# Second convolution of a spectral kernel: VectorE's chains on PSUM operands, SBUF sums on GpSimd, filters spread by DMA

## The chip, the core and the metric

The kernel runs on one core of one Trainium2 chip. The metric is the device time of one execution in microseconds (us); less is better.

## What is computed

The input x has 2 sequences of 3008 rows and 256 channels, in fp32. Three layers follow each other, and only the last one's result is handed out:

```python
X = np.fft.rfft(x, axis=1)
F = (filt_r + 1j * filt_i)[None, :, :]
y = np.fft.irfft(X * F, n=x.shape[1], axis=1).astype(np.float32)

x = y.reshape(6016, 256)
gate = 1.0 / (1.0 + np.exp(-(x @ w_gate)))        # 256 -> 1536
x = (gate * (x @ w_val) @ w_out).astype(np.float32)

h = x @ w_in                                      # 256 -> 2048
out = (h * (1.0 / (1.0 + np.exp(-1.702 * h))) @ w_out2).astype(np.float32)
```

## The kernel before

The Fourier transform of length 3008 = 47 x 64 is done as products with small tables. A convolution (class `Conv`) handles one sequence in 8 groups `g` of 32 channels, each group in two halves; a half is a chunk `j` = 2g + u with 16 channels, 16 chunks in all. For the second sequence (`b` = 1) its steps are:

- `a1(g)` (line 519): TensorE multiplies x with the table of length 47, in eight small matmuls of `four` (line 324), into PSUM banks 3 and 6. VectorE transposes both banks (line 526) into `a`. `highs` (ScalarE, 528) and `lows` (VectorE, 530) split `a` into a high and a low part `ap`, because a product in full precision is made of three matmuls (`mm3`, lines 124 to 126: high by high, high by low, low by high).
- `c1(j)` (532): the table of length 64, into bank 7. ScalarE copies the bank into `v` with real and imaginary halves exchanged (539, 540), VectorE multiplies the bank by the real filter into `y` (542), GpSimd multiplies `v` by the signed imaginary filter (543).
- `c1_sum(j)` (546): `y + v` on VectorE (548), high part `yp` on ScalarE (550), low part on VectorE (554).
- `d1(j)` (566): the inverse table of length 64, from `yp` into bank 7 again, and a transpose on VectorE into `z` (572).
- `e1(g)` (574): the inverse table of length 47, into banks 3 and 6, two transposes on VectorE into `tt` (408) and stores to memory.

`load_f(g)` (346) loads a group's two filters into partitions 0 to 63. `spread_f(j)` (394) copies each chunk's filters to partitions 64 to 127 on ScalarE (398), and `sign_f(j)` (400) multiplies the imaginary one by a table of signs on GpSimd (403).

This convolution is done inside 20 units of the second layer. A unit (loop at line 1194, `t` = 2, 3 and `f` = 2 to 11) takes one tile of 512 tokens and 128 columns of the hidden layer: six matmuls of the gate into one of PSUM banks 0 to 2, a sigmoid on ScalarE (1214), six of the value into another, their product on VectorE into `sg` (1247), a split into high part `g` (ScalarE, 120) and low part (GpSimd, 121), and six matmuls of `s12_back` (691) into banks 4 and 5, pushed back by two units (`depth`). Unit u carries `c1(u-1)`, `d1(u-2)`, and in alternation `a1` (even units) or `e1` (odd units).

Beside it the same units prepare what the third and later stages need: sums of the gate's weights (`combine_w1`, 1050, by `sum_ahead`), the split of tile 3 (657, 663), and the seven sums and differences of two later tiles ("forms", class `Forms`, 1083), each with a high part on ScalarE and a low part.

Each engine takes its instructions in the order in which this code lists them (`manual_schedule`, line 1181), and SyncE (SP) issues nearly all transfers from one queue, in that order as well.

Of the kernel before, what the change touches and what calls it, by code (L numbers as in the profile page):

```python
# [89 lines left out]
def kernel(  # L90
# [241 lines left out]
    class Conv:  # L332
        def __init__(self, b, fx, ff, fw):
            self.b, self.fx, self.ff, self.fw = b, fx, ff, fw
            self.x, self.f, self.st, self.z = {}, {}, {}, {}
            self.pa, self.pz, self.py = {}, {}, {}
            self.two = set()
            self.highs, self.lows = [], []
# [7 lines left out]
        def load_f(self, g):  # L346
            t = [self.ff.tile([P, 32, K1], F32, tag=f"f{i}", name=f"f{i}") for i in range(2)]
            gs = slice(g * 32, (g + 1) * 32)
            if self.b:
                for i in range(2):  # L350
                    nc.sync.dma_start(out=t[i][:64], in_=fd[i, :, gs])
            else:
                nc.sync.dma_start(out=t[0][:64], in_=fd[0, :, gs])
                for h in range(2):
                    hs = slice(g * 32 + h * 16, g * 32 + h * 16 + 16)
                    nc.sync.dma_start(out=t[1][h * 64:(h + 1) * 64, :16], in_=fd[1, :, hs])
# [163 lines left out]
        def a1(self, g):  # L520
            banks = ps[3], ps[6]
            x = self.x[g]
            four(enumerate(banks), tbl("t1"), lambda r, k: x[64 * r:64 * r + N1P, k], N1P)
            for u in range(2):
                a = self.fw.tile([P, 16, 32], F32, tag="a", name="a", bufs=2)
                nc.vector.transpose(a.rearrange("p c k -> p (c k)"), banks[u])
                ap = self.pair([P, 16, K1], "ap", 4)
                self.highs.append(lambda ap=ap, a=a: nc.scalar.activation(out=ap[0], in_=a[:, :, :K1], func=AF.Copy))
                self.st[2 * g + u] = ap
                self.lows.append(lambda ap=ap, a=a: nc.vector.tensor_sub(ap[1], a[:, :, :K1], ap[0].bitcast(F32)))  # L530

        def c1(self, j):
            g, u = divmod(j, 2)
            px = ps[7][:, :384]
            mm3(px, tbl3("t2"), self.st[j], True, True)
            pxv = px.rearrange("p (c k) -> p c k", k=K1)
            fr, fi = (t[:, u * 16:u * 16 + 16] for t in self.f[g])
# [3 lines left out]
            y = self.fw.tile([P, 16, K1], F32, tag="y", name="y", bufs=2)  # L541
            nc.vector.tensor_mul(y, pxv, fr)  # L542
            nc.gpsimd.tensor_mul(v, v, fi)
            self.st[j] = y, v

        def c1_sum(self, j):
# [3 lines left out]
            nc.scalar.activation(out=yp[0], in_=y, func=AF.Copy)  # L550
            self.st[j] = yp

            def low():
                nc.vector.tensor_sub(yp[1], y, yp[0].bitcast(F32))  # L554

            self.lows.append(low)

        def low(self):
            if self.lows:
                self.lows.pop(0)()  # L560
# [5 lines left out]
        def d1(self, j, bank=7):  # L566
# [7 lines left out]
        def e1(self, g):  # L574
# [475 lines left out]
    def combine_w1(f, n, v, r, eng=nc.vector):  # L1050
# [22 lines left out]
        def lo(k):  # L1073
            nc.vector.tensor_sub(dst[k][1], r[:, k], dst[k][0].bitcast(F32))  # L1074
# [8 lines left out]
    class Forms:  # L1083
# [41 lines left out]
        def inplace(self):  # L1125
            sub = nc.vector.tensor_sub
# [39 lines left out]

    cur = np_
# [4 lines left out]
    def sum_ahead(f, u):  # L1172
        if not ahead:
            ws = new_parts()[0].bitcast(F32).rearrange("p a (b m) -> p a b m", m=P)
            ahead.update({k: combine_w1(k, 1, ws[:, 0:1], ws[:, 1:2]) for k in range(PRE)})
        ahead[f][u]()

    for f in range(PRE):
        for u in range(5):
            at_unit(4 + (5 * f + u) * 4 // 5, lambda f=f, u=u: sum_ahead(f, u))  # L1180
# [12 lines left out]
    pre = []  # L1193
    for t in range(2, 4):
        for f in range(FK, FC1):
            pg, pv = front_bank(), front_bank()
            m = tiles[t][3]
            c = unit - 1 if 0 <= unit - 1 < NCH else None
            a = 0 if unit == 1 else unit // 2 if unit and unit % 2 == 0 and unit // 2 < 8 else None
            if c is not None and unit > 2:  # L1200
                conv.c1(c)
            if unit == 3:
                conv.c1_sum(1)
                conv.low()
# [6 lines left out]
            if unit != 2:  # L1211
                conv.high()
            sg = work.tile([P, 512], F32, tag="sg", name="sg")[:, :m]
            nc.scalar.activation(out=sg, in_=pg[:, :m], func=AF.Sigmoid)
            if unit != 2:
                conv.high()
            if unit == 2:
                conv.c1(0)
                conv.high()
                conv.high()  # L1220
                ended[0](0)
                conv.low()
                ended[0](1)
            elif unit == 3:
                conv.d1(0, 3)
                conv.c1_sum(2)
                conv.low()
            elif unit > 3:
                if c is not None:
                    conv.c1_sum(c)  # L1230
                    if a is not None:
                        conv.low()
                if 0 <= unit - 2 < NCH:
# [549 lines left out]
```

## Time and profile before

| | |
|---|---|
| runs | 1160.48 us median of 3 (1160.44 to 1161.47) |
| profiled execution | 1162.36 us, of which the span is 1160.5 us |
| TensorE (PE) busy | 1135.2 us, 98% of the span |
| VectorE (DVE) busy | 724.0 us, 62% |
| ScalarE (ACT) busy | 657.7 us, 57% |
| GpSimd (POOL) busy | 415.6 us, 36% |

The span is the time from the first to the last instruction of the profiled execution. The 20 units lie between about 172 and 313 us; the first convolution lies before 60 us, and the rest is matmul stages. "L542" is line 542 of the kernel. An engine's idle time is put down to whatever it waited for last.

### The profile page before, as it was taken

The page shows a single profiled execution, that of the slowest core. Times are in us where ns is not written, and L with a number is a line of the kernel's source. Part 1 is how long each engine was busy: PE and PEld are TensorE (multiplying, and loading weights), DVE is VectorE, ACT ScalarE, POOL GpSimd, SP SyncE. Part 2 cuts the span into 40 slices and gives each one's busy share as a digit, 9 for nine tenths or more (in the row PEclk, how much of TensorE's full clock was granted, in tenths as well). Part 3 has the DMA queues.
Part 4 walks back from the last instruction along what each step waited for, and adds up shares of the span by engine and source line. Part 5 has one row for each costly group of instructions (what it writes and reads, how often), then busy time and mean ns, then how long its engine had stood idle before and what let it go on. Part 6 is the DMA issues. An engine that isn't in the chain of part 4 may idle for free.

```text
span 1160.5 us, 14600 instructions
## 1 busy us (share of the span) xinstructions
PE 1135.2 (98%) x5072; PEld 907.5 (78%) x5072; DVE 724.0 (62%) x1193; ACT 657.7 (57%) x1253; POOL 415.6 (36%) x341
## 2 busy tenths in 40 slices
PE   9999998889999999999999999999999999999998
PEld 4378885656778788888888878888888888888887
DVE  6989985998688855688688789623333333233211
ACT  4555555555455654556566576656556556555554
POOL 4810004445433221221121122255454455554443
PEclk9999998999999999999999999999999999999999
DMA  9755245255210030026137351020020200200000
GB/s 206 192 186 169 91 143 143 74 115 98 73 55 1 1 109 1 1 88 110 49 127 240 128 163 60 1 73 1 7 67 1 71 1 1 73 1 1 37 1 35
DMA packets 80170, 86.75 MB, mean 75 GB/s; under 512 B 38304, under 2 KB 51104, under 8 KB 80096
## 3 DMA queue, kind: packets, MB, share of 16 engines
q1 hardware_dynamic: 78128, 82.88, 25.3%
q10 hardware_dynamic: 1968, 2.94, 0.7%
q8 instruction: 40, 0.66, 0.2%
q14 instruction: 34, 0.28, 0.1%
HBM read 54.08 MB, written 30.93 MB: 73 GB/s over the span
## 4 chain that ended last, share of the span: by engine, by line
PE 87%; DVE 6%; DMA 3%; issue 2%; ACT 1%; SPq 0%; POOL 0%; DVEq 0%; POOLq 0%; ACTq 0%
PE ps L124 28%; PE ps L125 28%; PE ps L126 28%; DMA x<-in_xd_dram 1%; PE ps L324 1%; DMA f<-in_fd_dram 1%; DVE yp L554 1%; PE ps L485 1%; DVE yp L1102 0%; DVE sx L1074 0%; DVE y L542 0%; DMA tabs<-in_tab_dram 0%; PE ps L441 0%; DVE tt L408 0%; DVE yp L1057 0%
## 5 line engine op out<-in xcount | busy, mean ns | idle before, releaser
L121 POOL TENSOR_TENSOR g<-sg,g 128x512 fp32r<-128x512 f32 (+1 forms) x68 | 89.8, 1320 | 372.7 <-ACT g L120 366.8
L1635 POOL TENSOR_TENSOR g<-sg,g 128x512 fp32r<-128x512 f32 (+1 forms) x117 | 149.9, 1294 | 172.2 <-ACT sg L1632 169.6
L1711 DVE TENSOR_TENSOR ps<-ps,tabs 128x512 f32<-128x512 f32 (+1 forms) x48 | 33.1, 689 | 214.8 <-PE ps L126 214.8
L124 PE MATMUL ps<-yp,wg 128*128 128x512 f32 (+1 forms) x382 | 151.1, 396 | 0.0
L125 PE MATMUL ps<-yp,wg 128*128 128x512 f32 (+1 forms) x382 | 149.2, 391 | 0.0
L126 PE MATMUL ps<-yp,wg 128*128 128x512 f32 (+1 forms) x382 | 149.1, 390 | 0.0
L1631 ACT ACTIVATE g<-ps 128x512 fp32r<-128x512 f32 (+1 forms) x128 | 76.1, 594 | 85.0 <-DVE ps L1713 58.3
L125 PE MATMUL ps<-g,wo 128*128 128x512 f32 (+1 forms) x288 | 111.1, 386 | 0.2 <-POOL g L121 0.2
L124 PE MATMUL ps<-g,wo 128*128 128x512 f32 (+1 forms) x288 | 111.1, 387 | 0.1
L126 PE MATMUL ps<-g,wo 128*128 128x512 f32 (+1 forms) x288 | 110.7, 386 | 0.0
L1635 POOL TENSOR_TENSOR wo<-sg,wo 128x512 fp32r<-128x512 f32 (+1 forms) x59 | 75.7, 1292 | 84.0 <-ACT sg L1632 83.3
L1632 ACT ACTIVATE sg<-ps 128x512 f32<-128x512 f32 (+1 forms) x176 | 104.8, 595 | 1.1 <-POOL g L1635 0.8
L124 PEld LDWEIGHTS ps<-yp,wg 128*128 128x128 f32 x382 | 72.5, 190 | 27.3 <-issue 13.8
L126 PEld LDWEIGHTS ps<-yp,wg 128*128 128x128 f32 x382 | 72.4, 190 | 14.6
L125 PEld LDWEIGHTS ps<-yp,wg 128*128 128x128 f32 x382 | 72.4, 190 | 13.4 <-issue 0.2
L125 PE MATMUL ps<-g,wg 128*128 128x512 f32 (+1 forms) x192 | 74.1, 386 | 0.3 <-POOL g L1635 0.3
L124 PE MATMUL ps<-g,wg 128*128 128x512 f32 (+1 forms) x192 | 74.0, 385 | 0.0
L126 PE MATMUL ps<-g,wg 128*128 128x512 f32 (+1 forms) x192 | 74.0, 385 | 0.0
L1569 ACT ACTIVATE sg<-ps 128x480 f32<-128x480 f32 (+1 forms) x48 | 28.1, 586 | 71.6 <-DVE ps L1567 71.6
L120 ACT ACTIVATE g<-sg 128x512 fp32r<-128x512 f32 (+1 forms) x68 | 42.4, 623 | 40.2 <-DVE sg L1591 29.3
L124 PEld LDWEIGHTS ps<-g,wo 128*128 128x128 f32 x288 | 54.2, 188 | 11.8 <-issue 0.8
L1602 DVE TENSOR_TENSOR g<-ps,g 128x480 fp32r<-128x480 f32 (+1 forms) x48 | 32.4, 675 | 49.1 <-ACT g L1599 48.9
(302 smaller groups left out, 2828.8 us busy)
## 6 DMA issues: line engine op xcount, KB each, us to landing
yraw<-xscr SPq DMA_DIRECT2D x16, 512.0 KB, 4.2
yscr<-tt SPq DMA_DIRECT2D x56, 128.0 KB, 2.1
raw<-in_w_out_dram SPq DMA_DIRECT2D x14, 512.0 KB, 3.8
x<-in_xd_dram SPq DMA_DIRECT2D x32, 192.0 KB, 4.5
wscr<-wl SPq DMA_DIRECT2D x24, 256.0 KB, 2.2
xscr<-yraw SPq DMA_DIRECT2D x12, 512.0 KB, 3.0
wg<-wscr SPq DMA_DIRECT2D x24, 256.0 KB, 2.9
f<-in_fd_dram SPq DMA_DIRECT2D x23, 192.0 KB, 4.8
```

Of the source, the lines that this page charges most:

```text
L120: nc.scalar.activation(out=dst_hi, in_=src, func=AF.Copy)
L121: lo_eng.tensor_sub(dst_lo, src, dst_hi.bitcast(F32))
L124: nc.tensor.matmul(out=o, lhsT=w[0], rhs=x[0], start=first, stop=False, **kw)
L125: nc.tensor.matmul(out=o, lhsT=w[0], rhs=x[1], start=False, stop=False, **kw)
L126: nc.tensor.matmul(out=o, lhsT=w[1], rhs=x[0], start=False, stop=last, **kw)
L324: nc.tensor.matmul(out=o[c], lhsT=w[64 * r:64 * r + n], rhs=x(r, k), start=True, stop=True, tile_position=(64 * r, 64 * k),)
L1569: nc.scalar.activation(out=sgz, in_=z, func=AF.Sigmoid)
L1602: nc.vector.tensor_sub(g0[1], x, g0[0].bitcast(F32))
L1631: nc.scalar.activation(out=self.gp[0], in_=self.bank, func=AF.Gelu_apprx_sigmoid)
L1632: nc.scalar.activation(out=self.sg, in_=self.bank, func=AF.Gelu_apprx_sigmoid)
L1635: (nc.vector if self.own else nc.gpsimd).tensor_sub(self.gp[1], self.sg, self.gp[0].bitcast(F32))
L1711: nc.vector.tensor_add(y, x, s5[:, :n])
```

## The change

VectorE's chain of a chunk stays in PSUM. `c1` leaves the product with the real filter to `c1_real`, which writes it into c1's own bank; `c1_sum` adds `v` there; `c1_low` takes the low part from there. The product of gate and value stays in the value's bank, with its high part from there on ScalarE and its low part from there on VectorE (before: GpSimd, from SBUF). `d1` gets bank 3 in place of 7. The transposes of `a1` and `e1` are queued as `turns` and placed one by one between the other steps.

GpSimd gets the low parts of `ap`, the sums of weights, the low part of tile 3, and the forms with their low parts.

The filters: `load_i` loads a group's imaginary filter with its two halves in partitions 0 to 63 and 64 to 127, `sign_i` signs it in one operation on GpSimd, and `load_both` fills both halves of both filter tiles by DMA: the real one twice from memory, the signed one in four pieces from SBUF. `spread_f` and `sign_f` are gone, with their 32 copies.

The forms are no longer a list `pre` that is taken off step by step, but steps with fixed units: `at_unit` (end of a unit) and `at_copy` (behind the sigmoid). `depth` becomes 3 from unit 16 on, and the first set of the next stage runs one `back` less.

```diff
         def load_f(self, g):
...
+        def load_i(self, g):
+            t = self.ff.tile([P, 16, K1], F32, tag="fi", name="fi", bufs=2)
+            for h in range(2):
+                hs = slice(g * 32 + h * 16, g * 32 + h * 16 + 16)
+                nc.sync.dma_start(out=t[h * 64:(h + 1) * 64], in_=fd[1, :, hs])
+            self.fi[g] = t
+
+        def sign_i(self, g):
+            t = self.fi[g]
+            nc.gpsimd.tensor_mul(t, t, sgn.unsqueeze(1).to_broadcast([P, 16, K1]))
+
+        def load_both(self, g):
+            t = [self.ff.tile([P, 32, K1], F32, tag=f"f{i}", name=f"f{i}") for i in range(2)]
+            fi = self.fi.pop(g)
+            for k in range(2):
+                ks = slice(64 * k, 64 * k + 64)
+                nc.sync.dma_start(out=t[0][ks], in_=fd[0, :, g * 32:(g + 1) * 32])
                 for h in range(2):
+                    nc.sync.dma_start(out=t[1][ks, h * 16:h * 16 + 16], in_=fi[64 * h:64 * h + 64])
             self.f[g] = t
...
+        def first_high(self, a, j):
+            self.st[j] = ap = self.pair([P, 16, K1], "ap", 3)
+            nc.scalar.activation(out=ap[0], in_=a[:, :, :K1], func=AF.Copy)
+            self.lows.append(lambda eng: eng.tensor_sub(ap[1], a[:, :, :K1], ap[0].bitcast(F32)))
...
-            y = self.fw.tile([P, 16, K1], F32, tag="y", name="y", bufs=2)
-            nc.vector.tensor_mul(y, pxv, fr)
-            nc.gpsimd.tensor_mul(v, v, fi)
-            self.st[j] = y, v
+            nc.gpsimd.tensor_mul(v, v, self.f[g][1][:, u * 16:u * 16 + 16])
+            self.st[j] = pxv, v
+
+        def c1_real(self, j):
+            g, u = divmod(j, 2)
+            y = self.st[j][0]
+            nc.vector.tensor_mul(y, y, self.f[g][0][:, u * 16:u * 16 + 16])
...
+        def c1_low(self, j):
+            y, yp = self.st[j]
+            nc.vector.tensor_sub(yp[1], y, yp[0].bitcast(F32))
             self.st[j] = yp
...
-        def d1(self, j, bank=7):
+        def d1(self, j, bank=3):
...
             elif unit == 3:
-                conv.d1(0, 3)
-                conv.c1_sum(2)
-                conv.low()
-            elif unit > 3:
-                if c is not None:
+                sigmoid()
+                conv.d1(0, 7)
+            else:
+                conv.high()
+                sigmoid()
+                if c is not None and unit > 3:
+                    conv.c1_real(c)
                     conv.c1_sum(c)
-                    if a is not None:
-                        conv.low()
-                if 0 <= unit - 2 < NCH:
-                    conv.d1(unit - 2)
-            if 2 < unit < NCH:
-                conv.spread_f(unit)
-                conv.sign_f(unit, nc.gpsimd)
+                conv.turn()
+                conv.high()
+                if d is not None:
+                    conv.d1(d)
+                if c is not None and unit > 3:
+                    conv.c1_low(c)
...
-            nc.vector.tensor_mul(sg, pv[:, :m], sg)
+            nc.vector.tensor_mul(pv[:, :m], pv[:, :m], sg)
...
-            split(*gp, sg, nc.gpsimd)
+            nc.scalar.activation(out=gp[0], in_=pv[:, :m], func=AF.Copy)
...
+            nc.vector.tensor_sub(gp[1], pv[:, :m], gp[0].bitcast(F32))
             if unit > 3:
                 conv.low()
                 conv.low()
...
-            if odd == 0 and 1 < g + 1 < 8:
-                conv.load_f(g + 1)
+            if unit == 3 or odd == 0 and 2 <= g < 7:
+                conv.load_both(g + 1)
+            if unit == 0:
+                conv.load_i(2)
+            elif odd and g + 3 < 8:
+                conv.load_i(g + 3)
```

**VectorE, unit 5.** Before (y is the product with the real filter, tt and z are transposes, yp0_1945 the sums of weights, yp1_1961 the low part of tile 3):

```order
L542 TENSOR_TENSOR y_1968<-ps7_78,f0_1825 128x384
L408 STREAM_TRANSPOSE tt_1975<-ps3_74 128x512
L408 STREAM_TRANSPOSE tt_1975<-ps6_77 128x512
L548 TENSOR_TENSOR y_1968<-y_1968,v_1965 128x384
L572 STREAM_TRANSPOSE z_1927<-ps7_78 128x512
L1247 TENSOR_TENSOR sg_1988<-ps1_72,sg_1988 128x512
L554 TENSOR_TENSOR yp1_1992<-y_1968,yp0_1991 128x384
L661 TENSOR_TENSOR yp1_1961<-yraw_1753,yp0_1960 128x512
L1067 TENSOR_TENSOR yp0_1945<-yp0_1945 128x128
L1068 TENSOR_TENSOR yp0_1945<-yp0_1945 128x128
```

The same unit with the change:

```order
L414 STREAM_TRANSPOSE tt_1996<-ps3_74 128x512
L556 TENSOR_TENSOR ps7_78<-ps7_78,f0_1892 128x384
L560 TENSOR_TENSOR ps7_78<-ps7_78,v_1982 128x384
L414 STREAM_TRANSPOSE tt_1996<-ps6_77 128x512
L584 STREAM_TRANSPOSE z_1943<-ps3_74 128x512
L567 TENSOR_TENSOR yp1_2003<-ps7_78,yp0_2002 128x384
L1284 TENSOR_TENSOR ps1_72<-ps1_72,sg_1978 128x512
L1305 TENSOR_TENSOR g1_2023<-ps1_72,g0_2022 128x512
```

Five of the first ten rows have no PSUM operand, none of the eight; g's low part (L1305) has come to this engine, and the transpose of d1 (z) reads bank 3.

**TensorE, the same unit** (ap is a1's split, yp the filtered chunk). Before:

```order
L124 MATMUL ps7_78<-ap0_1903,tab0_1655 128x384
L125 MATMUL ps7_78<-ap1_1904,tab0_1655 128x384
L126 MATMUL ps7_78<-ap0_1903,tab1_1656 128x384
L324 MATMUL ps3_74<-z_1854,tabs_88 64x512 x2
L324 MATMUL ps6_77<-z_1854,tabs_88 64x512 x2
L124 MATMUL ps0_71<-yp0_608,wg0_83 128x512
L125 MATMUL ps0_71<-yp1_609,wg0_83 128x512
L126 MATMUL ps0_71<-yp0_608,wg1_84 128x512
L124 MATMUL ps0_71<-yp0_608,wg0_83 128x512
L125 MATMUL ps0_71<-yp1_609,wg0_83 128x512
L126 MATMUL ps0_71<-yp0_608,wg1_84 128x512
L124 MATMUL ps7_78<-yp0_1920,tab0_1655 128x16x24
```

With the change:

```order
L124 MATMUL ps7_78<-ap0_1926,tab0_1655 128x384
L125 MATMUL ps7_78<-ap1_1927,tab0_1655 128x384
L126 MATMUL ps7_78<-ap0_1926,tab1_1656 128x384
L324 MATMUL ps3_74<-z_1860,tabs_88 64x512 x2
L324 MATMUL ps6_77<-z_1860,tabs_88 64x512 x2
L124 MATMUL ps0_71<-yp0_608,wg0_83 128x512
L125 MATMUL ps0_71<-yp1_609,wg0_83 128x512
L126 MATMUL ps0_71<-yp0_608,wg1_84 128x512
L124 MATMUL ps0_71<-yp0_608,wg0_83 128x512
L125 MATMUL ps0_71<-yp1_609,wg0_83 128x512
L126 MATMUL ps0_71<-yp0_608,wg1_84 128x512
L124 MATMUL ps3_74<-yp0_1932,tab0_1655 128x16x24
```

The order is the same; d1 (last row) writes the bank that e1 has written, no longer the one that c1 has.

**SyncE, the start of the convolution** (x_1659 and x_1665 are groups 0 and 1 of x, f0 and f1 the filters, fi the imaginary one as loaded). Before, x's second group follows the four filter loads of these rows:

```order
L344 DMA x_1659<-in_xd_dram 48x1024 x2
L351 DMA f0_1662<-in_fd_dram 64x768
L351 DMA f1_1663<-in_fd_dram 64x768
L351 DMA f0_1666<-in_fd_dram 64x768
L351 DMA f1_1667<-in_fd_dram 64x768
```

With the change:

```order
L344 DMA x_1659<-in_xd_dram 48x1024 x2
L359 DMA fi_1662<-in_fd_dram 64x384 x2
L344 DMA x_1665<-in_xd_dram 48x1024 x2
L359 DMA fi_1668<-in_fd_dram 64x384 x2
L371 DMA f0_1692<-in_fd_dram 64x768
L373 DMA f1_1693<-fi_1662 64x384 x2
L371 DMA f0_1692<-in_fd_dram 64x768
L373 DMA f1_1693<-fi_1662 64x384 x2
L371 DMA f0_1701<-in_fd_dram 64x768
L373 DMA f1_1702<-fi_1668 64x384 x2
```

x's second group now stands behind two half-sized loads, and the filters proper behind both groups of x; the rows of L373 wait for GpSimd's signs.

## Rows read from the trace of the kernel before

**Rows 1.** Table of stretches.

```profile
core 0: us, PE busy (x) PEld busy (x) DVE busy (x) ACT busy (x) POOL busy (x), PEclk, DMA share, GB/s
175.00:180.00 5.00, 5.00 (x26) 3.27 (x25) 0.87 (x2) 1.41 (x4) 1.32 (x2) 1.00 1.06 196
180.00:182.20 2.20, 0.47 (x3) 0.04 (x1) 1.71 (x3) 1.44 (x3) 1.25 (x2) 1.00 1.00 308
182.20:189.40 7.20, 7.16 (x20) 4.55 (x21) 3.22 (x5) 3.04 (x7) 2.00 (x2) 0.53 0.39 126
189.40:210.00 20.60, 18.78 (x86) 12.51 (x86) 16.67 (x27) 13.38 (x28) 11.95 (x10) 1.00 0.33 84
210.00:267.70 57.70, 47.46 (x229) 32.07 (x227) 55.59 (x80) 31.26 (x67) 27.32 (x23) 1.00 0.43 96
267.70:271.20 3.50, 3.48 (x9) 2.94 (x10) 2.72 (x5) 2.76 (x6) 0.02 (x1) 0.54 0.88 263
271.20:314.00 42.80, 42.38 (x205) 31.02 (x204) 30.65 (x46) 21.43 (x41) 22.94 (x19) 1.00 0.42 82
```

**Rows 2.** TensorE's waits, 165 to 330 us: us in total, times, longest.

```profile
PE ps L124 <- DVE y L542: 10.7, 8, 2.2
PE ps L324 <- DMA x<-in_xd_dram: 1.8, 1, 1.8
PE ps L124 <- DVE z L572: 0.9, 1, 0.9
PE ps L125 <- DVE yp L554: 0.7, 2, 0.4
```

**Rows 3.** Timeline of TensorE, unit 5 and a later one: start us, us.

```profile
210.37 0.40 PE L125 MATMUL ps<-yp,wg 128*128 128x512 f32 x1
210.60 0.40 PE L126 MATMUL ps<-yp,wg 128*128 128x512 f32 x1
212.60 0.45 PE L124 MATMUL ps<-yp,tab 128*128 128x384 f32 x1 [1.61 <-DVE y L542]
212.89 0.34 PE L125 MATMUL ps<-yp,tab 128*128 128x384 f32 x1
...
248.70 1.09 PE L324 MATMUL ps<-x,tabs 48*64 48x512 f32 x8
```

**Rows 4.** Timeline of VectorE in unit 5.

```profile
208.98 1.77 DVE L1057 TENSOR_TENSOR yp<-wg,wg 128x512 f32<-128x512 f32 x1
...
212.00 0.55 DVE L542 TENSOR_TENSOR y<-ps,f 128x384 f32<-128x384 f32 x1
```

**Rows 5.** Timeline of GpSimd in unit 5.

```profile
208.60 1.60 POOL L121 TENSOR_TENSOR g<-sg,g 128x512 fp32r<-128x512 f32 x1
```

**Rows 6.** Groups, 175 to 325 us: busy us, mean ns, idle before.

```profile
L408 DVE STREAM_TRANSPOSE tt<-ps 128x512 f32<-128x512 f32 x16 | 10.4, 688 | 0.0
...
L548 DVE TENSOR_TENSOR y<-y,v 128x384 f32<-128x384 f32 x16 | 8.8, 553 | 0.1
L542 DVE TENSOR_TENSOR y<-ps,f 128x384 f32<-128x384 f32 x16 | 8.8, 551 | 10.5 <-ACT v L540 9.6 <-PE ps L324 0.9
...
L121 POOL TENSOR_TENSOR g<-sg,g 128x512 fp32r<-128x512 f32 x20 | 28.6, 1431 | 112.3 <-ACT g L120 112.3
L543 POOL TENSOR_TENSOR v<-v,f 128x384 f32<-128x384 f32 x16 | 18.4, 1153 | 7.0 <-ACT v L540 7.0
...
L539 ACT ACTIVATE v<-ps 64x384 f32<-64x384 f32 x16 | 7.8, 488 | 3.2 <-PE ps L126 2.9
```

**Rows 7.** Timeline of SyncE's queue, start of the convolution.

```profile
171.90 2.40 SPq L351 DMA_DIRECT2D f<-in_fd_dram  x4
174.35 1.51 SPq L344 DMA_DIRECT2D x<-in_xd_dram  x2
```

**Rows 8.** DMA issues, 174.33 to 176 and 200 to 290 us: us to landing.

```profile
x<-in_xd_dram SPq DMA_DIRECT2D x2, 192.0 KB, 7.4
...
x<-in_xd_dram SPq DMA_DIRECT2D x8, 192.0 KB, 3.7
```

More of the change, by code (lines that the diff above doesn't have):

```diff
@@ L334, in __init__ @@
             self.b, self.fx, self.ff, self.fw = b, fx, ff, fw
[L335 removed]
+            self.x, self.f, self.fi, self.st, self.z = {}, {}, {}, {}, {}
             self.pa, self.pz, self.py = {}, {}, {}
             self.two = set()
[L338 removed]
+            self.turns, self.highs, self.lows = [], [], []
         def load_x(self, g, halves=(0, 1)):
@@ L523, in a1, with turn_1, c1 @@
             four(enumerate(banks), tbl("t1"), lambda r, k: x[64 * r:64 * r + N1P, k], N1P)
[L524 to L532, printed above, removed]
+            self.turns += [lambda u=u: self.turn_1(g, u, banks[u]) for u in range(2)]
+        def turn_1(self, g, u, bank):
+            a = self.fw.tile([P, 16, 32], F32, tag="a", name="a", bufs=2)
+            nc.vector.transpose(a.rearrange("p c k -> p (c k)"), bank)
+            self.highs.append(lambda: self.first_high(a, 2 * g + u))
+        def first_high(self, a, j):
+            self.st[j] = ap = self.pair([P, 16, K1], "ap", 3)
+            nc.scalar.activation(out=ap[0], in_=a[:, :, :K1], func=AF.Copy)
+            self.lows.append(lambda eng: eng.tensor_sub(ap[1], a[:, :, :K1], ap[0].bitcast(F32)))
+        def c1(self, j, bank=7):
             g, u = divmod(j, 2)
-            px = ps[7][:, :384]
+            px = ps[bank][:, :384]
             mm3(px, tbl3("t2"), self.st[j], True, True)
             pxv = px.rearrange("p (c k) -> p c k", k=K1)
-            fr, fi = (t[:, u * 16:u * 16 + 16] for t in self.f[g])
             v = self.fw.tile([P, 16, K1], F32, tag="v", name="v", bufs=2)
@@ L580, in e1, with back, turn @@
             )
-            for h in range(2):
+            def back(h):
                 self.to_time(h, banks[h])
                 self.store(g, h)
+            self.turns += [lambda h=h: back(h) for h in range(2)]
+        def turn(self):
+            if self.turns:
+                self.turns.pop(0)()
     tiles = [(b, q, h, 512 if q < 2 else 480) for b in range(B) for q in range(3) for h in range(2)]
@@ L1165, in at_unit, with at_copy @@
         later.setdefault(u, []).extend(fns)
+    copies = {}
+    def at_copy(u, *fns):
+        copies.setdefault(u, []).extend(fns)
     cur = np_
@@ L1174, in sum_ahead @@
             ws = new_parts()[0].bitcast(F32).rearrange("p a (b m) -> p a b m", m=P)
-            ahead.update({k: combine_w1(k, 1, ws[:, 0:1], ws[:, 1:2]) for k in range(PRE)})
+            ahead.update({k: combine_w1(k, 1, ws[:, 0:1], ws[:, 1:2], nc.gpsimd, nc.gpsimd) for k in range(PRE)})
         ahead[f][u]()
@@ L1192 @@
     ends = {2 * g + 5: g for g in range(6)} | {16: 6, 18: 7}
-    pre = []
+    signs = {3: 2, 4: 3} | {2 * g - 3: g for g in range(4, 8)}
+    EXT = nc.gpsimd
     for t in range(2, 4):
@@ L1198, with sigmoid @@
             c = unit - 1 if 0 <= unit - 1 < NCH else None
+            sg = work.tile([P, 512], F32, tag="sg", name="sg")[:, :m]
+            def sigmoid():
+                nc.scalar.activation(out=sg, in_=pg[:, :m], func=AF.Sigmoid)
+                if t == 2 and f in (7, 9):
+                    split_y_hi(3, raw, nxt, f // 9)
+                for step in copies.pop(unit, ()):
+                    step()
             a = 0 if unit == 1 else unit // 2 if unit and unit % 2 == 0 and unit // 2 < 8 else None
-            if c is not None and unit > 2:
-                conv.c1(c)
+            d = unit - 2 if unit > 1 and unit - 2 < NCH else None
+            if unit > 2 and c is not None:
+                conv.c1(c, 3 if c == 2 else 7)
             if unit == 3:
                 conv.c1_sum(1)
-                conv.low()
+                conv.c1_real(2)
+                conv.c1_low(1)
             if a is not None and unit > 1:
@@ L1210 @@
                 s12_mm(t, f, cur, pg, 0, k)
[L1211 to L1216, printed above, removed]
+            conv.turn()
             if unit == 2:
+                conv.turn()
+                sigmoid()
                 conv.c1(0)
+                conv.c1_real(0)
                 conv.high()
@@ L1574 @@
             back()
-            back()
+            if not first_set:
+                back()
             spend(chores, rate[1])
```

126 lines of the change are left out of this document (62 added, 64 removed).

## The prediction

> **What bounds the kernel now.** I read the page first: TensorE is busy 98% of the span, so only time in which it stands still or runs slowly can be won. The table of stretches then says where that is: nearly all of it lies between 180 and 314 us, the 20 units with the second convolution [rows 1]. In each row the reader subtracts TensorE's busy time from the length: 1.73 + 0.04 + 1.82 + 10.24 + 0.02 + 0.42 = 14.3 us idle. [...]
>
> The waits of TensorE name the causes [rows 2]: 10.7 us in eight waits for line 542, VectorE's product of c1's PSUM bank 7 with the real filter; 1.8 us for a transfer of x; 0.9 and 0.7 us for a transpose and a low part. A wait also costs more than its entry. In [rows 3] the matmul before it starts at 210.60, the waiting one at 212.60; without the wait it would follow after 0.23, so 1.77 are lost where 1.61 are listed, and the next one follows after 0.29 instead of about 0.17 (384 of 512 columns of 0.23). That is 0.28 more for each of 12 waits, 3.4 us. **All that can be won there is 14.3 + 3.4 + 5.0 = 22.7 us.**
>
> Why is line 542 late? d1(u-2) writes bank 7, which c1(u-1) has filled just before, so it must wait until that product has been read. And VectorE comes late: it is busy 55.6 of 57.7 us between 210 and 267.7 [rows 1]. Its timeline shows why [rows 4]: line 1057, two SBUF operands, 512 columns, takes 1.77 us where 512 columns otherwise take 0.69 [rows 6], and ends at 210.75, 0.55 after GpSimd's line 121 has ended at 210.20 [rows 5]. Line 542, one operand in PSUM and one in SBUF, takes 0.55 in that timeline and 0.551 in the mean of 16 [rows 6], with GpSimd running beside several of them. So VectorE stretches when both inputs are in SBUF, and not otherwise.
>
> **The change, part by part, in the steady units (5 to 18).**
>
> *VectorE.* It keeps, per unit, c1_real, c1_sum, c1_low (0.55 each), the transpose of d1, two turns (transposes of a1 or e1), the value product and g's low part (0.69 each), all with at most one SBUF operand: 3 x 0.55 + 5 x 0.69 = 5.1 us. It loses the lows of a1, the sums of w1, the lows of y and the forms.
>
> *TensorE's unit.* 18 matmuls of 0.23, 6 of 0.17, one group of four-way matmuls of 1.09 [rows 3]: 6.2 us. So VectorE has 1.1 us to spare, and d1 no longer waits for c1's bank: it writes bank 3 and needs only the first turn. That one can start when VectorE has ended g's low part of the unit before, about 1.2 us into the unit, and ends at 1.9; d1 comes after c1, a1 and the gate product, at 0.5 + 1.1 + 1.4 = 3.0. Bank 3 is given back (transpose of d1) at 4.7, and a1 or e1 writes it at 6.7; bank 7 is given back by c1_low at 5.2, and c1 writes it at 6.2. No wait is left; the smallest margin is 1 us. I take the eight waits, two of the other short ones, and the second slow-clock stretch (which follows the longest wait) as gone.
>
> *GpSimd.* It gains the lows of a1 (two in every second unit) and the sums, and loses g's low part (20 x 1.43 in the stretch) and half of the sign products. With 1.15 per 384 columns [rows 6] a unit costs 1.15 + 1.15 + 0.6 = 2.9 us, and the fullest one (unit 10: product, two lows, two small sums, one form) 5 x 1.15 + 1.44 = 7.2 us if a 128-column sum took as much as a 384-column one, 5.7 us if it took a third. Between them I take the lower, in proportion to columns. Cost nothing; it is hidden under 6.2 us of TensorE. The product with the imaginary filter is queued behind these sums, c1_sum waits for it, and behind c1_sum stand the value product and the next turn; that cover is gone when a unit exceeds 6.2.
>
> *ScalarE.* It loses 32 filter copies and gets g's high part from PSUM; nothing waits on it longer than now.
>
> *SyncE's queue.* Per pair of units it had 4 stores, 2 loads of x, 2 of filters; now 4, 2, 2 loads of the raw imaginary part and 6 of load_both. At 0.6 us an issue [rows 7] these 14 take 8.4 of 12.4 us. load_both is put in the queue at unit 2g for a filter first used at 2g+3, and loads of x at 2g+1 for 2g+4, so a landing of 3.7 us [rows 8] is hidden by over a unit. Cost nothing.
>
> **The start (units 0 to 3).** The second a1 waited for x1, issued at 174.35 and landing 7.4 us later [rows 7, 8], because 768 KB of filters stood ahead of it. Now 192 KB do. At the 196 GB/s of the stretch before [rows 1] 576 KB are 2.9 us, at 308 they are 1.9; so x1 lands 1.9 to 2.9 earlier, against a standstill of 1.7. I charge 0.2 (bounds 0, and 1.7 if nothing is gained). With the standstill goes the slow clock behind it, 3.4 us; that is my choice, since rows show slow stretches only behind standstills of about 2 us.
>
> The filters of group 0 come later than now: raw part landed and signed by about 180, then four issues of 0.6 to the half that c1(0) needs, 3.7 us to land: about 185.5. TensorE ends c1(0) near 183.4 and two ScalarE copies of 0.49 [rows 6] follow, so GpSimd's product starts near 184.7. It may be 0.8 us late, but c1_sum(0) is the fifth operation of VectorE's chain. Cost nothing; bounds 0 and 3.7 (landing as slow as x1's).
>
> What then lasts longest is VectorE's own chain. Between c1(0) and d1(1) it has nine operations of 0.55 and four of 0.69, 7.7 us, after 1.0 us of copies; TensorE has 24 x 0.23 + 9 x 0.17 = 7.1 us there. So **a new wait of about 1.7 us stands before the products of units 2 and 3** (the accumulator banks 4 and 5, or d1(1)), 2.0 with what a wait costs besides. Bounds: 0, since starts in the timeline follow closer than durations, and 5.4 if a slow clock of 3.4 follows. I take 2.0.
>
> [...]
>
> *The end.* The forms now end on GpSimd; the last low (form 6) falls in unit 19, some 3 us before the product with it starts. Nothing, with bounds -0.4 (the idle left after 271) and +1.
>
> **Sum:** 22.7 - 0.2 - 2.0 = 20.5 us. The profiled execution took 1162.4 us, so 1141.9 by its own time; the median of the runs shown stands 1.9 below it, and 1160.5 - 20.5 = **1140.0 us**.
>
> **Rivals.**
>
> 1. *The filters come late.* If load_both's parts land after 7.4 us like x1, VectorE's chain of units 2 and 3 shifts by 3.7, and a standstill that long brings the slow clock, 3.4: 1140 + 7.1 = 1147. For it: the first dozen transfers queue behind each other, and the second of load_both waits on GpSimd. Against it: 3.7 us as soon as the queue is emptier. Chance 0.12.
>
> 2. *VectorE stays the slower engine.* Were additions with one PSUM operand stretched by GpSimd by 0.3 each, four of them per unit, VectorE would need 6.3 to 6.7 us and TensorE wait up to 0.5 in 14 units: 1147. The same holds if GpSimd's fullest units pass 6.2. Against it: line 542 does not stretch. Chance 0.07. Were the stretch 0.8, as line 1057's, no gain would be left (8.3 us a unit); 0.03 for ending within 0.2%, which is about what a measurement of this kernel can tell from no change.
>
> 3. *Slower: the transfers run out.* Each transfer waits until the eighth before it in SyncE's queue has landed. Fourteen per pair of units at a mean landing of L take 14 L / 8. Up to L = 7.1 us that is below the 12.4 us of two units; above it a1 waits for x. To lose the 20.5 us again over seven groups takes 2.9 us each, L = 8.8; at 9.3 it would be 16.3 us a pair, 27 us lost, 1167 us. For it: 7.4 us at the start, and 576 KB more per group. Against it: 3.7 us later, with the DMA engines busy 0.43 of the time. Chance 0.04.
>
> **How the numbers follow.** Forecast 0.74, with 1137 (the unit 2 and 3 wait not there, and the end's bound) to 1145 (slow clock there); rivals 0.12, 0.07 and 0.03, 0.04. The range 1137 to 1149 takes in the first two rivals and leaves out the others. Faster 0.93, the same 0.03, slower 0.04.
>
> **What would show it.** Right: TensorE's waits on line 556 (once 542) in units 5 to 13 gone; VectorE's c1_sum, c1_low and g's low near 0.55, 0.55 and 0.69 while GpSimd runs; clock 1.00 from 190 on; one or two waits, under 2 us together, near 185 to 192. Wrong: waits of the four-way matmuls for x or of c1_sum for GpSimd in the steady units; a low clock in units 2 to 4; VectorE over 6 us busy per unit.

## The result: 1139.47 us, and the profile after

The changed kernel takes 1139.47 us (median of 4 runs, 1139.31 to 1140.85), the kernel before, beside it on the same chip, 1160.46 us (4 runs, 1156.79 to 1161.47): a ratio of 0.9827, 95% interval 0.9805 to 0.985. The profiled execution took 1140.85 us with a span of 1139.0 us. The forecast was 1140.0, with 1137 to 1149 as its range.

The table of stretches of the changed kernel, cut as in [rows 1] (columns: TensorE, its weight loads, VectorE, ScalarE and GpSimd busy, each with its instructions; clock; DMA share; GB/s):

```profile
175.00:180.00 5.00, 5.00 (x26) 3.25 (x25) 3.27 (x6) 1.80 (x3) 0.96 (x1) 1.00 1.02 204
180.00:182.20 2.20, 2.20 (x14) 0.92 (x13) 2.16 (x4) 1.05 (x2) 1.15 (x2) 1.00 0.44 108
182.20:189.40 7.20, 6.57 (x30) 5.05 (x29) 6.15 (x12) 3.94 (x8) 2.02 (x2) 1.00 0.79 215
189.40:210.00 20.60, 20.27 (x99) 14.05 (x98) 16.62 (x30) 11.74 (x25) 12.13 (x15) 1.00 0.75 193
210.00:267.70 57.70, 57.70 (x289) 41.23 (x289) 43.58 (x74) 30.50 (x64) 31.86 (x40) 1.00 0.83 179
267.70:271.20 3.50, 3.50 (x17) 2.93 (x17) 3.39 (x7) 0.98 (x2) 2.19 (x2) 1.00 0.16 35
271.20:314.00 42.80, 42.74 (x199) 33.96 (x198) 27.75 (x57) 19.97 (x43) 16.45 (x14) 1.00 0.29 84
```

TensorE stands still for 0.63 + 0.33 + 0.06 = 1.0 us where it was 14.3, and the clock is 1.00 throughout. The gain lies in these units and not elsewhere: `a1`'s first matmul starts at 177.79 us before and at 178.19 with the change, the first copy of line 1545 (now 1595), which belongs to the stage behind them, at 313.9 and 292.1, and its last copy at 663.2 and 641.8. The DMA share between 210 and 267.7 has nearly doubled, 0.43 to 0.83. Of TensorE's waits [rows 2] two short ones are left (165 to 330 us):

```profile
PE ps L124 <- DVE yraw L732: 0.5, 1, 0.5
PE ps L124 <- DVE yp L567: 0.3, 1, 0.3
```

The groups of VectorE and GpSimd that answer to [rows 6] (busy us, mean ns | idle before):

```profile
L1305 DVE TENSOR_TENSOR g<-ps,g 128x512 fp32r<-128x512 f32 x20 | 13.8, 691 | 12.2 <-ACT g L1286 12.2
...
L560 DVE TENSOR_TENSOR ps<-ps,v 128x384 f32<-128x384 f32 x16 | 9.0, 564 | 2.2 <-POOL v L550 1.1
L556 DVE TENSOR_TENSOR ps<-ps,f 128x384 f32<-128x384 f32 x16 | 8.6, 539 | 1.0 <-ACT v L549 1.0
L567 DVE TENSOR_TENSOR yp<-ps,yp 128x384 fp32r<-128x384 f32 x16 | 8.6, 539 | 0.6
...
L550 POOL TENSOR_TENSOR v<-v,f 128x384 f32<-128x384 f32 x16 | 16.2, 1015 | 34.4 <-ACT v L549 18.4 <-issue 9.8 <-DMA f<-fi 4.5
L540 POOL TENSOR_TENSOR ap<-a,ap 128x384 fp32r<-128x384 f32 x12 | 12.1, 1010 | 5.8 <-DMA yscr<-tt 3.1 <-ACT ap L539 2.0 <-DMA x<-in_xd_dram 0.8
```

VectorE's operations with a PSUM operand keep their price while GpSimd runs, 0.54 to 0.56 us for 384 columns and 0.69 for 512, where [rows 6] has 0.55 and 0.69; and GpSimd is faster than before: 1.02 us for 384 columns, 1.15 in [rows 6]. The DMA issues, 200 to 290 us (KB each, median us to landing), for [rows 8]:

```profile
x<-in_xd_dram SPq DMA_DIRECT2D x10, 192.0 KB, 3.4
f<-in_fd_dram SPq DMA_DIRECT2D x10, 192.0 KB, 4.3
f<-fi SPq DMA_DIRECT2D x20, 96.0 KB, 4.1
```

### The profile page after: what moved, and what is told of

The parts are those of the page before. It is cut to its first block, busy times and chain, and to the rows that moved or that the text cites. A ratio compares the mean times of both kernels' runs of the same rounds, so it can differ in the third digit from the quotient of the medians.

```text
span 1139.0 us, 14619 instructions
## 1 busy us (share of the span) xinstructions
PE 1129.3 (99%) x5072; PEld 906.4 (80%) x5072; DVE 696.7 (61%) x1173; ACT 641.5 (56%) x1221; POOL 407.3 (36%) x353
## 4 chain that ended last, share of the span: by engine, by line
PE 94%; issue 2%; DVE 1%; POOL 1%; DMA 1%; ACT 1%; SPq 0%; ACTq 0%; POOLq 0%; DVEq 0%
PE ps L124 31%; PE ps L126 30%; PE ps L125 30%; PE ps L324 2%; PE ps L491 1%; DMA t<-in_tab_dram 0%; PE ps L447 0%; DMA f<-in_fd_dram 0%; PE ps L493 0%; POOL f L399 0%; DVE yp L1121 0%; DVE z L500 0%; POOL y L484 0%; POOL v L468 0%; POOL y L478 0%
## 5 line engine op out<-in xcount | busy, mean ns | idle before, releaser
L1686 POOL TENSOR_TENSOR g<-sg,g 128x512 fp32r<-128x512 f32 (+1 forms) x117 | 149.9, 1295 | 172.2 <-ACT sg L1683 169.6
L121 POOL TENSOR_TENSOR g<-sg,g 128x480 fp32r<-128x480 f32 (+1 forms) x48 | 61.1, 1273 | 263.0 <-ACT g L120 263.0
L124 PEld LDWEIGHTS ps<-g,wo 128*128 128x128 f32 x288 | 54.0, 188 | 12.4 <-DVE yraw L732 1.4
L1682 ACT ACTIVATE wo<-ps 128x512 fp32r<-128x512 f32 (+1 forms) x64 | 38.1, 595 | 44.1 <-DVE ps L1764 29.9
L125 PEld LDWEIGHTS ps<-g,wo 128*128 128x128 f32 x288 | 54.0, 188 | 10.8 <-POOL g L121 0.6
```

Of the source, the lines that this page charges most:

```text
L121: lo_eng.tensor_sub(dst_lo, src, dst_hi.bitcast(F32))
L124: nc.tensor.matmul(out=o, lhsT=w[0], rhs=x[0], start=first, stop=False, **kw)
L125: nc.tensor.matmul(out=o, lhsT=w[0], rhs=x[1], start=False, stop=False, **kw)
L1682: nc.scalar.activation(out=self.gp[0], in_=self.bank, func=AF.Gelu_apprx_sigmoid)
L1686: (nc.vector if self.own else nc.gpsimd).tensor_sub(self.gp[1], self.sg, self.gp[0].bitcast(F32))
```

## The experiments

**Was VectorE late, or was it the bank?** The kernel before, d1 of the units from 4 on in bank 3:

```diff
-                    conv.d1(unit - 2)
+                    conv.d1(unit - 2, 3)
```

> The kernel before, with d1 of units 4 to 17 in bank 3 instead of c1's bank 7, and nothing else. Theory (VectorE comes late, whichever bank it is): on VectorE the transposes that free bank 3 stand right behind the product of line 542, so the eight waits of 10.7 us stay and get 0.5 to 0.7 longer each: 1160 to 1166 us. Rival (the shared bank was the cause): the eight waits are gone, 1145 to 1150 us.

1165.35 us, ratio 1.0065 (1.0042 to 1.0087): somewhat slower, as expected. TensorE's waits moved to the next transposes:

```profile
PE ps L124 <- DVE tt L408: 10.4, 7, 2.4
PE ps L124 <- DVE a L526: 4.0, 2, 2.6
```

The bank alone wins nothing; whatever VectorE has to free there is freed late.

**The sums alone, and both together.** The kernel before with its two-SBUF sums and forms on GpSimd, at their old places, and the same with bank 3:

```diff
-                nc.vector.tensor_add(r[:, 0], a21, a22)
+                rest.tensor_add(r[:, 0], a21, a22)
...
-            ahead.update({k: combine_w1(k, 1, ws[:, 0:1], ws[:, 1:2]) for k in range(PRE)})
+            ahead.update({k: combine_w1(k, 1, ws[:, 0:1], ws[:, 1:2], nc.gpsimd, nc.gpsimd) for k in range(PRE)})
...
-                split_y_lo(3, raw, nxt, f // 9, vec)
+                split_y_lo(3, raw, nxt, f // 9, nc.gpsimd)
```

> The kernel before with one part of the change alone: the sums of weights, the low part of tile 3 and the forms with their low parts go from VectorE to GpSimd, at the places where they stood; 26 instructions, all with two SBUF operands. They took 30.8 us of VectorE's 139 us between 175 and 314 (lines 1057 to 1074, 661, 1102, 1129 to 1141). Theory (VectorE comes late to line 542 because of work in SBUF that GpSimd stretches): the waits for line 542 fall from 10.7 us to under 4, the second slow-clock stretch is gone, and the time is 1148 to 1154 us; the start's wait for x stays. Rival (where it stands in the queue decides: the work now stands in GpSimd's queue ahead of the product with the imaginary filter, so the sum c1_sum waits for GpSimd and VectorE is late all the same): waits of 8 us or more stay, for line 542 or for GpSimd, and the time is 1156 us or more. The work is complete.

> As the run with the sums on GpSimd alone, and d1 of the units from 4 on in bank 3 in place of 7, the second part of the change. On the kernel before, bank 3 alone won nothing (1165.35 us): the waits moved to the next transpose. Theory (the bank matters only once VectorE is in time; then c1 and d1 no longer pass one bank between them): less than 1.5 us of waits left in the units 5 to 18, and 1 to 4 us below the run with the sums alone. Rival (the shared bank never matters; only VectorE's lateness does): within 1 us of the run with the sums alone, or above it, with the waits again moved to the transposes. The work is complete.

1157.85 us, ratio 0.9971 (0.996 to 0.9981), and with bank 3 1160.08 us, 0.999 (0.9979 to 1.0), which can hardly be told from the kernel before. In both the time came out as the rival had it. In the run with the sums alone VectorE's load did fall, from 46.26 to 32.52 of the 50 us from 200 to 250, and the waits for line 542 fell below 4 us as the theory said; but new waits came in their place. TensorE's waits (165 to 330 us):

```profile
PE ps L124 <- DVE z L572: 4.7, 6, 1.3
PE ps L124 <- DVE y L542: 3.9, 5, 2.3
...
PE ps L124 <- ACT sg L1214: 1.7, 1, 1.7
```

From 175 to 314 us TensorE stands still 13.4 us, where it was 14.3: half as long as before between 210 and 267.7 us (5.0 for 10.2), but 4.1 us after 271.2, where it was 0.4. The waits of VectorE and of ScalarE in that run, 175 to 314 us, say why:

```profile
DVE y L542 <- ACT v L540: 19.2, 13, 5.0
DVE y L548 <- POOL v L543: 12.1, 10, 2.7
```

```profile
ACT yp L550 <- DVE y L548: 19.3, 13, 3.2
...
ACT xk L1097 <- POOL yraw L1141: 3.7, 1, 3.7
```

The sum (548) waits for GpSimd's product (543), and GpSimd's timeline of unit 5 shows what that stands behind:

```profile
207.66 1.59 POOL L121 TENSOR_TENSOR g<-sg,g 128x512 fp32r<-128x512 f32 x1
209.21 1.28 POOL L1057 TENSOR_TENSOR yp<-wg,wg 128x512 f32<-128x512 f32 x1
210.58 0.46 POOL L1064 TENSOR_TENSOR yp<-yp 128x128 f32<-128x128 f32 x1
211.12 0.46 POOL L1065 TENSOR_TENSOR yp<-yp 128x128 f32<-128x128 f32 x1
211.53 1.01 POOL L543 TENSOR_TENSOR v<-v,f 128x384 f32<-128x384 f32 x1
```

g's low part, which becomes ready at the unit's end, then the sums; GpSimd is busy only 34.73 of the 50 us from 200 to 250. So VectorE's load is part of the lateness, and with half of it gone the order in the queues holds VectorE up. The 4.1 us after 271.2 are such a case too: ScalarE's high parts of the forms (line 1097) stand ahead of its copies of c1 and of a sigmoid, and wait for the forms on GpSimd, which stand behind g's low part. The change gives the forms fixed units; that part was not run by itself.

**g's low part.** The changed kernel with the product of gate and value in SBUF and g's low part on GpSimd again, and then the same with the two low parts of a1 ahead of it:

```diff
-            nc.vector.tensor_mul(pv[:, :m], pv[:, :m], sg)
+            nc.vector.tensor_mul(sg, pv[:, :m], sg)
...
-            nc.scalar.activation(out=gp[0], in_=pv[:, :m], func=AF.Copy)
+            nc.scalar.activation(out=gp[0], in_=sg, func=AF.Copy)
...
-            nc.vector.tensor_sub(gp[1], pv[:, :m], gp[0].bitcast(F32))
+            nc.gpsimd.tensor_sub(gp[1], sg, gp[0].bitcast(F32))
```

> The changed kernel, with the product of gate and value in SBUF and its low part on GpSimd again. Theory: VectorE loses 0.69 us per unit and nothing of it is stretched, GpSimd gains 1.3 us and passes 6.2 us only in one or two units: 1139 to 1142 us. Rival (GpSimd becomes the chain): c1_sum waits for the product with the imaginary filter in most units and TensorE with it, 1145 us or more.

The second run's edit to that:

```diff
-            nc.gpsimd.tensor_sub(gp[1], sg, gp[0].bitcast(F32))
             if unit > 3:
                 conv.low()
                 conv.low()
+            nc.gpsimd.tensor_sub(gp[1], sg, gp[0].bitcast(F32))
```

> The same kernel as the one with g's low part on GpSimd, with one thing changed: in the units from 4 on, GpSimd does the two low parts of a1 ahead of g's low part instead of behind it; the same instructions, the same load. Theory (order in GpSimd's queue: the low parts of a1 stood behind an instruction that can start only when the unit has ended): the six waits of c1's second matmul for GpSimd's ap, 16.5 us there, are gone, the clock is 1.00 from 200 us on, and the time is 1139 to 1146 us; somewhat over the changed kernel because g's low part, at the unit's end, now stands ahead of GpSimd's product with the imaginary filter. Rival (GpSimd has too much to do, or its work with two SBUF operands stretches VectorE's): 1155 us or more, with waits for other work of GpSimd in place of those. The work is complete.

1174.99 us, ratio 1.0121 (1.0099 to 1.0143), slower than the kernel before, where I had expected 1139 to 1142; and with the same instructions in the other order 1150.71 us, 0.991 (0.9893 to 0.9927). TensorE's waits of the first, and GpSimd's timeline at 222 us:

```profile
PE ps L125 <- POOL ap L540: 16.5, 6, 3.1
```

```profile
222.82 1.26 POOL L1305 TENSOR_TENSOR g<-sg,g 128x512 fp32r<-128x512 f32 x1 [3.60 <-ACT g L1286]
224.04 1.93 POOL L540 TENSOR_TENSOR ap<-a,ap 128x384 fp32r<-128x384 f32 x2
```

c1's second matmul needs a1's low part (line 540), which stood behind g's (line 1305). Between 200 and 250 us GpSimd was busy 27.57 us, VectorE 21.49, and the clock was 0.83. The rival named GpSimd's queue, but another wait: that of c1_sum. In the second run these six waits are gone, and what is left is the link of the sums run, on VectorE (175 to 314 us):

```profile
DVE ps L560 <- POOL v L550: 21.2, 13, 2.6
```

```profile
PE ps L124 <- DVE yp L567: 5.7, 8, 1.3
```

I had allowed this some microseconds; TensorE's waits for line 567 behind it (second row) came to 5.7 us, and 1139 to 1146 was too low. The two kernels ran on two chips, on which the kernel before took 1161.16 and 1160.34 us; so of the 24.3 us between them up to 0.8 may be the chips.

**The filters.** The changed kernel with the filters loaded, copied on ScalarE and signed on GpSimd as before, x's second group behind them:

```diff
     conv.load_x(0)
-    conv.load_i(0)
+    conv.load_old(0)
+    conv.load_old(1)
     conv.load_x(1)
-    conv.load_i(1)
...
+            if 2 < unit < NCH:
+                conv.spread_f(unit)
+                conv.sign_f(unit, nc.gpsimd)
             for k in range(2):
                 s12_mm(t, f, cur, pv, 1, k)
```

> The changed kernel, with the filters loaded, copied by ScalarE and signed by GpSimd as before, and x1 loaded behind them as before. Theory: the standstill before the second a1 and the slow clock come back, 5.1 us, and the steady units stay without waits, since ScalarE has room: 1144 to 1146 us. Rival (the filters' way through the DMA is what clears the steady units too): TensorE waits in units 5 to 15 again, above 1148 us.

Then the same with the sign at the unit's end, behind a1's low parts:

```diff
-                conv.sign_f(unit, nc.gpsimd)
...
             if unit > 3:
                 conv.low()
                 conv.low()
+            if 2 < unit < NCH:
+                conv.sign_f(unit, nc.gpsimd)
```

> The same kernel as the one with the filters in the old way (copies on ScalarE, signs on GpSimd), with the sign product of units 3 to 15 moved from the unit's middle to its end, behind the two low parts of a1; nothing else. That kernel took 1156.3 us. Theory (order in GpSimd's queue: the low parts stood behind a product that waits for ScalarE's copies): the six waits of c1's second matmul for GpSimd's ap, 9.3 us there, are gone; what stays is the start, 1.7 us of waiting for x and the low clock behind it, about 5 us; 1144 to 1147 us. Rival (the 32 copies on ScalarE cost as much by themselves, through the sigmoid and the high parts behind them): 1152 us or more, with waits for ScalarE's work. The work is complete.

1156.26 us, ratio 0.9955 (0.994 to 0.9971), where the theory had 1144 to 1146, and 1142.71 us, 0.9855 (0.9827 to 0.9883), below the 1144 to 1147 expected. TensorE's waits of the first, and GpSimd's timeline at 203 us:

```profile
PE ps L125 <- POOL ap L557: 9.3, 6, 1.7
```

```profile
203.54 1.00 POOL L370 TENSOR_TENSOR f<-f,tabs 128x384 f32<-128x384 f32 x1 [2.81 <-ACT f L365]
204.49 1.94 POOL L557 TENSOR_TENSOR ap<-a,ap 128x384 fp32r<-128x384 f32 x2
```

GpSimd idles 2.81 us for ScalarE's copy while a1's low parts stand behind the sign. Moving one instruction per unit behind them takes 13.6 us off by the medians. Part of that is the clock, which differed between executions of one kernel: the only execution of the first with a mean granted clock of 1.00 took 1152.60 us, the two of the second 1141.72 and 1141.83, 10.8 us less. So it is the order and not the filters' way through the DMA that clears the steady units. The 32 copies cost next to nothing there: TensorE stands still 0.3 us between 210 and 267.7 in the second run. The rest over 1139.47, 3.2 us, holds a wait of 1.7 us for x at the start and, in the two other executions (1143.60 and 1147.21 us), a lower mean clock of 0.998 and 0.997.

**Sums and low parts back on VectorE**, in the changed kernel (likewise in `inplace` and `sum_ahead`):

```diff
-        def low(self, eng=nc.gpsimd):
+        def low(self, eng=nc.vector):
...
-    EXT = nc.gpsimd
+    EXT = nc.vector
```

> The changed kernel, with a1's lows, the sums of weights, tile 3's low part and the forms on VectorE again. Theory: VectorE gets about 10 us of work back between 200 and 250 us, GpSimd little to do, so few stretches; VectorE passes 6.2 us in the units with weight sums and TensorE waits there: 1142 to 1150 us. Rival (the PSUM operands alone were enough): 1139 to 1141 us.

1149.36 us, ratio 0.9916 (0.9899 to 0.9932). As much as expected, though VectorE is busy only 41.08 of 50 us:

```profile
PE ps L125 <- DVE ap L540: 7.7, 6, 1.5
```

The low parts of a1 stand behind g's low part again, now in VectorE's queue; I had expected the load of the weight sums to be the cause. These sums also show what GpSimd does to them: with GpSimd busy only 11.13 of the 50 us, the instruction that took 1.77 us before [rows 4] takes 0.685 on the same engine:

```profile
L1076 DVE TENSOR_TENSOR yp<-wg,wg 128x512 f32<-128x512 f32 x2 | 1.4, 685 | 0.0
```

**y in SBUF**, in the changed kernel:

```diff
-            y = self.st[j][0]
-            nc.vector.tensor_mul(y, y, self.f[g][0][:, u * 16:u * 16 + 16])
+            px, v = self.st[j]
+            y = self.fw.tile([P, 16, K1], F32, tag="y", name="y", bufs=2)
+            nc.vector.tensor_mul(y, px, self.f[g][0][:, u * 16:u * 16 + 16])
```

> The changed kernel, with the product with the real filter written to SBUF again, so that the sum and the low part of y have two SBUF inputs. Theory (two SBUF inputs are stretched by GpSimd): both go from 0.55 to 0.75 or 0.9 us in the mean, VectorE to 5.5 to 5.8 us per unit, and TensorE waits a little in some units: 1140 to 1144 us. Rival (the place of the operand does not matter, only the amount of work): both stay at 0.55 us, 1139 to 1140 us.

1143.19 us, ratio 0.9867 (0.9852 to 0.9882), 3.7 us more than the changed kernel by the medians (4.6 by the ratios), within the theory's range. The sum with two SBUF operands is stretched more than I had it, 1077 ns in the mean for 564, the low part less, 633 for 539:

```profile
L562 DVE TENSOR_TENSOR y<-y,v 128x384 f32<-128x384 f32 x16 | 17.2, 1077 | 4.3 <-POOL v L550 4.0
```

What was measured of the stretch, then: 1077 ns here for 564 with one of the two operands in PSUM, and for 512 columns 1.77 us with GpSimd beside [rows 4, 5] for 0.685 in the run above.

**The start.** The kernel before with x's second group loaded ahead of the filters, and then also with the first two ScalarE filter copies at the end of unit 1 in place of 0:

```diff
     conv.load_x(0)
+    conv.load_x(1)
...
-    conv.load_x(1)
```

> The kernel before, with the second group of x loaded ahead of the filters. Theory: x1 lands in time, the standstill of 1.8 us before the second a1 and the slow clock behind it (3.4 us) are gone: 1155 to 1156 us. Rival: the filters now land later, ScalarE's first copy of them holds up the sigmoid of unit 1 and with it VectorE's transposes, so the second a1 waits just as long for its banks: 1159 to 1162 us.

```diff
-            if unit == 0:
-                conv.spread_f(0)
-                conv.sign_f(0, nc.gpsimd)
...
                 conv.low()
+                conv.spread_f(0)
+                conv.sign_f(0, nc.gpsimd)
                 conv.spread_f(1)
```

> The kernel before with x's second group loaded ahead of the filters, as in the earlier run, and the first two filter copies of ScalarE with their sign moved from the end of unit 0 to the end of unit 1, so that the sigmoid of unit 1 no longer stands behind copies that wait for a transfer. Theory (two releasers, either of which alone holds up the second a1): its wait falls from 1.9 us to under 0.8, the clock of 182.2 to 190 us is 1.00, and 1.2 + 3.4 + 0.3 us are won against 1160.5: 1155 to 1157 us. Rival (the low clock there does not hang on the standstill, or a third releaser stands behind): 1159 us or more with a clock below 0.8 in that stretch. The waits for the product with the real filter, in units 5 to 13, stay at some 10 us either way. The work is complete.

1162.06 us, ratio 1.0018 (1.0006 to 1.0029); and 1157.19 us, 0.9971 (0.9958 to 0.9985). With x early the wait is there under another name:

```profile
PE ps L324 <- DVE a L526: 1.9, 1, 1.9
```

a1's banks were not free: the sigmoid of unit 1, and with it VectorE's transposes, stood behind a filter copy that waited for its load (ScalarE idle for 3.69 us). With the copy moved the wait is gone, the clock of 182.2 to 189.4 is 1.00 (0.57 in the first run), and 3.2 us are won, not the 4.9 expected: the waits for line 542 grew from 10.7 to 12.1 us.

**The two waits that are left.** The changed kernel with the two additions of line 732 ahead of c1_real(0):

```diff
                 conv.c1(0)
+                ended[0](0)
+                ended[0](1)
                 conv.c1_real(0)
...
-                ended[0](0)
                 conv.low(vec)
-                ended[0](1)
```

> The changed kernel, with the two additions that free banks 4 and 5 (line 732) ahead of c1_real(0) in VectorE's unit 2, where it waits for ScalarE. Theory: TensorE's wait of 0.5 us for them goes and VectorE's chain gets up to 1 us shorter: 1138.0 to 1139.0 us. Rival: the chain to d1(1) ends as late as now, 1139.3 to 1139.6 us.

1139.02 us (five runs, 1137.85 to 1140.45), ratio 0.9814 (0.9794 to 0.9834): the wait for line 732 is gone, the one for line 567 is 0.7, and the time can't be told from the changed kernel's.

## Why the prediction was right, point by point

- **What could be won: right.** Of the 22.7 us, 1.0 us of standing still and some 0.6 (twice 0.28) are left, so 21.1 came; the spans differ by 1160.5 - 1139.0 = 21.5, the medians by 21.0, and the forecast was 20.5. No run shows the 5.0 of that sum by itself: it is an estimate from the clock column of [rows 1], 7.2 x 0.47 + 3.5 x 0.46. What the trace of the kernel before shows is that in the first of these two stretches, with a clock of 0.53, matmuls of 512 columns start 0.43 us apart, where [rows 3] has 0.23 (210.37 and 210.60); with the change the clock is 1.00 in both.

```profile
186.07 0.63 PE L124 MATMUL ps<-yp,wg 128*128 128x512 f32 x1
186.50 0.63 PE L125 MATMUL ps<-yp,wg 128*128 128x512 f32 x1
```

- **"Why is line 542 late?": only in part.** The step named VectorE's stretched work in SBUF and the shared bank. The sums alone won 3.2 us, the bank alone nothing, and both together 1.0, at the edge of what can be measured. With that work gone, the run with the sums showed a ring that, with the forms' places, holds up TensorE nearly as long (13.4 us of standing still for 14.3): GpSimd's product waits behind what becomes ready at the unit's end, VectorE's sum waits for it, ScalarE's high part, filter copies and copies of the next c1 follow, and line 542 waits for those (19.2 us above). The stretch is one link (3.7 us in the run with y in SBUF). The time was right because the change breaks all the links at once, and the forecast priced their end, TensorE's waits. In part that is luck: that g's low part leaves GpSimd, which is worth 11 to 36 us in the two runs that put it back, stands in the forecast only as 0.69 us more for VectorE and less load for GpSimd.
- **VectorE: right.** 43.58 of 57.7 us is 4.8 us for a unit of 6.4, against 5.1 and 6.2. The smallest margin was to be 1 us; the timeline of unit 5 has c1_low's end at 206.57 and c1's next matmul at 207.50, 0.93 us (VectorE, then TensorE):

```profile
205.32 0.67 DVE L584 STREAM_TRANSPOSE z<-ps 128x512 f32<-128x512 f32 x1
206.01 0.56 DVE L567 TENSOR_TENSOR yp<-ps,yp 128x384 fp32r<-128x384 f32 x1
...
207.84 0.69 DVE L1305 TENSOR_TENSOR g<-ps,g 128x512 fp32r<-128x512 f32 x1 [0.67 <-ACT g L1286]
209.23 0.72 DVE L534 STREAM_TRANSPOSE a<-ps 128x512 f32<-128x512 f32 x1 [0.71 <-PE ps L324]
```

```profile
207.50 0.33 PE L124 MATMUL ps<-ap,tab 128*128 128x384 f32 x1
```

  The first turn waits for its matmuls (last row of VectorE), not for g's low part, as I had it.
- **0.55 us for operands in PSUM: right in effect, on a weak reading.** The forecast takes 0.55 for c1_sum in PSUM, which is what line 548 took with two SBUF operands. But the 0.553 of line 548 [rows 6] is a mean with one execution of 1.06 us in it; its median is 0.514. So the sum got 0.05 us longer in PSUM (median 0.567); the product (0.550 to 0.534) and the low part (0.555 to 0.539) got shorter, and the three together take only 0.02 us more. The waits behind that chain came out below the forecast (0.5 and 0.3 us), so nothing was lost by it.
- **GpSimd: cost right, reason wrong.** The fullest unit has 1.02 + 2 x 1.01 + 2 x 0.46 + 1.11 = 5.1 us, for 5.7. I let its cover end "when a unit exceeds 6.2". Four runs lost 10 to 36 us against the changed kernel with GpSimd busy 28 to 36 of 50 us or, with the low parts on VectorE, 11. What counted was what stood ahead in its queue and when that became ready; and I had counted a1's low parts as load alone, with no price for TensorE's wait for them, though c1 needs them at once.
- **SyncE's queue and the DMA: right.** x lands in 3.4 us and the filters' parts in 4.1 to 4.3, for 3.7, far from the 7.1 at which rival 3 begins. Its rule on the queue fits the traces: of the 335 transfers of SyncE's queue before and the 383 with the change none was issued before the eighth ahead of it had landed, while 23 and 26 were issued before the seventh had.
- **The start: size right, cause half.** x late was one of two releasers; the change removes both, as ScalarE's copies are gone. The filters came as reckoned: GpSimd's first product at 185.41 (I had 185.5), not seen by the sum, which VectorE reaches at 187.38. The new waits are where they were put (line 732 for bank 4 or 5, line 567 for d1(1)) and a little over half as large: 1.0 us of standing still between 182.2 and 210, for 1.7.
- **Rivals.** Filters late, VectorE still slower, transfers running out: none occurred.

## What to carry to other kernels

An engine that works in order can be half idle and still be the bound, as GpSimd was with 27.57 of 50 us busy in the slowest run: for each instruction, ask what stands ahead of it in the queue and when the last of that becomes ready, before counting the engine's load. Moving work to an idle engine paid here only at a place where nothing late stood ahead and nothing urgent behind; the same instructions in another order were worth some 11 to 14 and some 24 us. And a wait can have two releasers, as that of the second a1 had (1.8 us for x, and 1.9 us for a transpose with x early): the list names the last one, so removing that alone may only change the name.

## What the runs showed of the hardware

The clock after the standstill at 180 to 182 us is not fixed by its length. Four executions waited 1.7 to 2.1 us for x at that place; their granted clock over 182.2 to 189.4 was 0.53 (before), 0.76 (sums alone), 0.76 and 1.00 (the two with the old filters): from about half the full clock to all of it. The last of them:

```profile
180.00:182.20 2.20, 1.04 (x8) 0.45 (x8) 2.16 (x5) 1.80 (x4) 0.03 (x1) 1.00 1.01 360
182.20:189.40 7.20, 6.59 (x31) 4.66 (x27) 5.46 (x11) 5.55 (x12) 3.35 (x4) 1.00 0.32 92
```

A fifth stood still 1.9 us there for a transpose (the kernel before with x first): 0.57. In the profiled executions without a standstill of over 1 us at that place the clock was 1.00. So the 3.4 us that the forecast counted for it are those of the execution shown, and what else decides it stays open. Open is also whether the order alone, with VectorE's chains left in SBUF, would have done, and what the forms' fixed units, the deeper `depth` and the shorter first set are worth; none of these was tried.
